# A fp32 attention and two feed-forward nets on TensorE: output places, token places and deferred sums held by other times, and more steps with seven products

## The chip, the cores and the metric

The kernel runs on one core of a Trainium2 chip. The metric is the device time of the whole kernel in microseconds (us), the median of several runs. All times below are in us unless marked ns.

## The reference

Attention over channels (a 256 x 256 score matrix) on 6016 tokens, then two feed-forward nets with 256 -> 2048 -> 256 features, all in fp32:

```python
qn = q / (norm(q, axis=1) + 1e-06);  kn = k / (norm(k, axis=1) + 1e-06)
s = kn.T @ qn / tau                                   # 256 x 256
a = exp(s - s.max(-1));  a /= a.sum(-1) + 1e-09
x = v @ a                                             # 6016 x 256
h = x @ moe_w_in;   x = (h / (1 + exp(-h))) @ moe_w_out
h = x @ moe2_w_in;  out = maximum(0.01 * h, h) @ moe2_w_out
```

## The kernel before

**Stages.** The first 60 us read q and k, make the score matrix and the softmax, and fold it into the first weights, so that net one works on v itself. Net one (`moe` 1) and net two (`moe` 2) fill the rest. Their tokens are cut into six pairs of halves, `tpairs`: five of 2 x 512 and one of 2 x 448. For each net and each pair, written (net, pair) as (2,1), there are eight steps `s`; a step makes two of the sixteen blocks of 128 hidden features for both halves of the tokens, and adds them, times w_out, into four PSUM banks `ps_y`, one for each pair of an output block `m` and a token half.

**Products.** TensorE (PE) multiplies fp32 values as high and low parts: each product is three matmuls, hi x hi, hi x lo and lo x hi, called a triplet here. The first layer of a step (`product`, L477, into ps_a, ps_b and ps_d) makes 2 x 2 blocks with seven products M1 to M7 instead of eight, with sums on VectorE (DVE) and ScalarE (ACT): DVE's `da` (L561) adds into ps_d, `d22` (L581) makes a block of hidden values `hs`. After the activation (ACT L488, L490) each block is split: ACT casts the high part `gh` (L123), DVE subtracts for the low part `gl` (`lows`, L504).

The second layer (L650) of a plain step has eight products (`l2`). In a step with seven (`l2_seven`) the hidden blocks are first combined into sums T1 and T2 (DVE, L600) and T3 and T4 (transfers on POOL's queue that add in memory, L613), and P1 to P7 take them with w_out or with sums of w_out blocks (`wsh`, `wsl`). P2, P3, P4 and, in pairs whose last step is plain, P5 go into ps_y directly. P1, P6, P7 and otherwise P5 are chained over the steps of a batch in the bank ps_x, which DVE copies or adds to E1, E2, E3 or E5 in SBUF (`keep`, L712) and later adds into ps_y (`close`, L723). `SECOND` and `BATCHES` (L65, L66) say which steps of a pair are seven and how they are batched; without an entry in `BATCHES` a pair of net two takes `SECOND`.

**End of a pair.** `finish` (L732) brings each of the four banks to SBUF as `o`: in net one with an addition or a copy (L740, L743) and a transfer to `y_d` in memory (L745); in net two by a transpose (L747) and four transfers each to the output (L753), on SP's queue, sixteen for a pair.

**Places.** `hs`, `gh`, `gl`, the tokens `xf`, `xh`, `xl`, the loaded `v_raw`, `E` and `o` lie in a common set of places of 128 x 512 fp32 in SBUF. `take` pops the first of the list `free`, and who is done puts a place back at its end. An instruction that gets a place still being read waits for the reader.

**Order.** A planner (L1178 to the end of the kernel function) sets the order on all engines: every piece is a `Work` with an engine, a cost, the works it waits for, a due time `at` in steps, an earliest step `release`, and the number of places it needs (`homes`, `spare`). It takes the work that can start first by its own estimate, with a delay `LATE` after each engine, and looks at the first 48 of each queue. Works on the queue "none" have no instruction; they take or free places. `new_x` (L158) takes the places of the next pair's tokens and gives back those of the pair before the last.

Of the kernel before, what the change touches and what calls it, by code (L numbers as in the profile page):

```python
# [15 lines left out]
P = 128  # L16
# [3 lines left out]
def attention_moe_kernel(  # L20
# [44 lines left out]
    SECOND = ((0, 1, 2, 3), (4, 5, 6))  # L65
    BATCHES = {(1, 3): ((2, 4), (5, 6)), (1, 4): ((0, 1), (2, 4), (5, 6)), (1, 5): ((0, 1), (2, 4), (5, 6))}  # L66
# [91 lines left out]
    def new_x(qi, n=7):  # L158
        if qi > 1:
            for a in (xh, xl):  # L160
                free.extend(x[0] for x in a.pop(qi - 2) if x)
        xf[qi] = [take(F32, "xf") for _ in range(n)] + [None] * (7 - n)
        xh[qi], xl[qi] = [None] * 7, [None] * 7
# [567 lines left out]

    def finish(moe, p, m, half):  # L732
# [3 lines left out]
        free.append(i)  # L736
        if moe == 1:
            if batches(moe, p):
                name = last_add(moe, p, m, half)
                nc.vector.tensor_tensor(out=o[:, :n], in0=ps, in1=kept[p, name][1][:, :n], op=ALU.add)  # L740
                fed_on(p, name, own_fifth(moe, p))
            else:
                nc.vector.tensor_copy(out=o[:, :n], in_=ps)  # L743
            y_d[p, m, half] = dram.tile([P, n], F32, tag=f"y{p}{m}{half}", name="y_d")
            nc.sync.dma_start(out=y_d[p, m, half], in_=o[:, :n])  # L745
            return
        nc.vector.transpose(out=o[:, :n], in_=ps)  # L747
# [7 lines left out]
    def drop_x(qi):  # L755
        for a in (xh, xl):
            free.extend(x[0] for x in a.pop(qi) if x)

    with tc.manual_schedule():
# [365 lines left out]
        WIDTHS = {"i": 7 * HG, "o": FG * C, "s": 3 * P, "f": 3 * P, "a": P}  # L1125
# [22 lines left out]
        ENDING = ("P1", "P5", "P6", "P2", "P7", "P3", "P4")  # L1148
# [7 lines left out]
        def open_more():  # L1156
            decode.close()
            more_pool[0] = ctx.enter_context(tc.tile_pool(name="spool", bufs=1))
            last_pool = ctx.enter_context(tc.tile_pool(name="hpool", bufs=1))
            spots.update({i: last_pool for i in range(HOMES, HOMES + 2)})  # L1160
            free.extend(range(HOMES, HOMES + 2))
# [28 lines left out]
        rel, last_x = {}, None  # L1190
# [19 lines left out]
        def prepare_out(g, dep, at):  # L1210
            s1 = dep
            for x in (2 * g, 2 * g + 1):
# [8 lines left out]
            return done  # L1221
# [45 lines left out]
        def tokens(qi):  # L1267
# [3 lines left out]
            old = [o for (a, kk), o in ONES.items() if kk // SS == qi - 2]  # L1271
            new = Work("none", 0, lambda eng: new_x(qi, 4), old, release=k - 0.5, homes=4, spare=2)
            got = []
            for x, (kc, half) in enumerate(blocks):
                if qi < NP:
                    ld = Work("sp", 0.4, lambda eng, a=(qi, kc, half): load_v(*a), [new], release=k + x // 2, homes=1, spare=6)
# [4 lines left out]
            def form(i, deps, keeps=False, frees=()):  # L1281
                h = Work("act", sc(n), lambda eng: x_hi(qi, i, eng), deps, homes=2, spare=6)
# [52 lines left out]
        def first(k):  # L1335
# [11 lines left out]
            if qi == 2 * NP - 1 and s == 0:  # L1347
                Work("none", 0, lambda eng: drop_x(2 * NP - 2), [o for (a, kk), o in ONES.items() if kk // SS == qi - 1])
# [13 lines left out]
            def split(form, deps, free_deps=()):  # L1362
                h = Work("act", sc(n), lambda eng: cast(step, form, eng), deps, homes=1)
# [23 lines left out]
            else:  # L1387
# [7 lines left out]
                ready["T2"] = split("T2", [t2])  # L1395
                ready["T3"] = split("T3", [t3])
# [4 lines left out]
        def add(k):  # L1401
# [5 lines left out]
            wdeps = W2.get(g, []) if moe == 2 else W2.get(("first", s, "s"), W2["first", g])  # L1407
# [76 lines left out]
            if s == SS - 1:  # L1484
                for m in range(KC):
                    for half in range(2):
                        o = Work("dve", tt(n), lambda eng, a=(moe, p, m, half): finish(*a), ends[qi, m, half] + extra.get((qi, m, half), []), homes=1, at=k + 1.5 + half / 2)
                        FIN[qi, m, half] = after_fin[m, half] = o
# [16 lines left out]
        while left:  # L1505
            best = None
            for e, q in queues.items():
                q[:48] = [o for o in q[:48] if o.end is None]
                mine = None
                for o in q[:48]:  # L1510
# [16 lines left out]
            clock[e] = t + cost  # L1527
# [41 lines left out]
```

## Time and profile before

| | before |
|---|---|
| median of 3 runs | 1013.74 us (1013.54 to 1014.42) |
| the profiled execution | 1013.32 us |
| its span, first to last instruction | 1011.3 us |
| mean granted TensorE clock | 0.998 |
| busy: PE, DVE, ACT, POOL | 996.6, 836.1, 768.3, 161.1 us |

The profiled execution is one run; its span leaves out what lies before the first and after the last instruction. A busy time is the union of an engine's instructions. Two matmuls overlap in the profile (each lasts 0.39 us, but the next starts 0.23 us later), so the pace of PE is read from starts and its halts from longer distances between starts. A line of busy time by stage has the stretch, its length, then the busy time and number of instructions of PE, PEld (loads of weights, which overlap PE), DVE, ACT and POOL, the granted clock (1.00 is full speed), the share of the DMA engines and GB/s; in the chain of waits each line is a start, a length and what ran or was under way, "SPq" being SP issuing a transfer.

### The profile page before, as it was taken

How to read it: one execution, taken by the hardware profiler on the slowest of the kernel's cores; microseconds unless marked ns; L12 is line 12 of the kernel's file. 1: busy time of each engine (PE TensorE's matmuls, PEld its weight loads, DVE VectorE, ACT ScalarE, POOL GpSimd, SP SyncE). 2: the span in 40 equal slices, each digit the busy share in tenths (PEclk: the TensorE clock that was granted, in tenths of full speed). 3: DMA queues.
4: the chain of work that ended last, by engine and by line, in shares of the span. 5: the costliest groups of instructions: out<-in, count | busy, mean ns of one | idle time of the engine just before them, and what ended most of it. 6: DMA issues, size and time to landing. Idle time of an engine off the chain costs nothing.

```text
span 1011.3 us, 13654 instructions
## 1 busy us (share of the span) xinstructions
PE 996.6 (99%) x4450; PEld 830.1 (82%) x4450; DVE 836.1 (83%) x1432; ACT 768.3 (76%) x1427; POOL 161.1 (16%) x207
## 2 busy tenths in 40 slices
PE   8999999999999999999999999999999999999997
PEld 7878888887888888888998888888788788888996
DVE  5889887988898778888878888888788888888876
ACT  6888756877787777777876887887787797787774
POOL 2300000000001231211334221221120221121220
PEclk9999999999999999999999999999999999999999
DMA  9734625556548455423789643542533533442533
GB/s 352 292 107 133 150 67 170 177 168 162 208 172 193 116 104 94 98 46 78 198 229 312 142 84 74 95 82 68 100 64 83 96 71 78 84 81 43 91 55 61
DMA packets 152088, 128.38 MB, mean 127 GB/s; under 512 B 97488, under 2 KB 114384, under 8 KB 152016
## 3 DMA queue, kind: packets, MB, share of 16 engines
q1 hardware_dynamic: 120944, 74.93, 25.1%
q0 software_dynamic: 27360, 52.11, 25.0%
q10 hardware_dynamic: 3712, 0.46, 0.3%
q8 instruction: 35, 0.57, 0.2%
q14 instruction: 37, 0.30, 0.1%
HBM read 60.95 MB, written 31.85 MB: 92 GB/s over the span
## 4 chain that ended last, share of the span: by engine, by line
PE 85%; DMA 5%; DVE 4%; SPq 2%; ACT 2%; issue 1%; DVEq 0%; ACTq 0%; POOLq 0%
PE ps_y L650 31%; PE ps_a L477 22%; PE ps_x L650 12%; PE ps_d L477 11%; PE ps_b L477 5%; PE ps_h L477 3%; DMA k_raw<-in_k_dram 2%; SPq L753 2%; DVE gl L504 1%; PE w_ps L384 1%; DMA q_raw<-in_q_dram 1%; DMA w_raw<-in_moe_w_in_dram 1%; DMA hs<-hs 1%; DMA out_dram<-o 1%; SPq L791 0%
## 5 line engine op out<-in xcount | busy, mean ns | idle before, releaser
L504 DVE TENSOR_TENSOR gl<-hs,gh 128x512 fp32r<-128x512 f32 (+1 forms) x558 | 363.9, 673 | 74.5 <-ACT gh L123 66.0
L123 ACT CAST gh<-hs 128x512 fp32r<-128x512 f32 (+1 forms) x558 | 324.1, 610 | 6.7 <-DMA hs<-hs 0.8
L650 PE MATMUL ps_y<-gh,wol 128*128 128x512 f32 (+1 forms) x462 | 178.5, 386 | 0.5 <-DVE wol L355 0.5
L650 PE MATMUL ps_y<-gh,woh 128*128 128x512 f32 (+1 forms) x462 | 178.6, 387 | 0.2 <-DVE ps_y L723 0.2
L650 PE MATMUL ps_y<-gl,woh 128*128 128x512 f32 (+1 forms) x462 | 178.6, 387 | 0.0
L613 POOL DMA_DIRECT2D hs<-hs x116 | 100.9, 912 | 483.1 <-DVE gl L504 144.6
L477 PE MATMUL ps_a<-xh,wch 128*128 128x512 f32 (+1 forms) x352 | 137.3, 390 | 3.5 <-DVE ps_d L561 2.3
L477 PE MATMUL ps_a<-xl,wch 128*128 128x512 f32 (+1 forms) x352 | 135.7, 385 | 0.0
L477 PE MATMUL ps_a<-xh,wcl 128*128 128x512 f32 (+1 forms) x352 | 135.6, 385 | 0.0
L650 PEld LDWEIGHTS ps_y<-gh,wol 128*128 128x128 f32 x462 | 86.7, 188 | 17.7 <-DVE wol L355 0.9
L650 PEld LDWEIGHTS ps_y<-gh,woh 128*128 128x128 f32 x462 | 86.7, 188 | 17.2 <-DVE ps_y L723 0.5
L650 PEld LDWEIGHTS ps_y<-gl,woh 128*128 128x128 f32 x462 | 86.7, 188 | 16.9 <-DVE gl L504 0.3
L581 DVE TENSOR_TENSOR hs<-ps_a,c 128x512 f32<-128x512 f32 (+1 forms) x88 | 59.5, 676 | 37.4 <-PE ps_a L477 36.4
L600 DVE TENSOR_TENSOR hs<-hs 128x512 f32<-128x512 f32 (+1 forms) x116 | 78.1, 673 | 10.3 <-ACT hs L490 5.0
L477 PEld LDWEIGHTS ps_a<-xh,wch 128*128 128x128 f32 x352 | 66.0, 188 | 22.0 <-DVE ps_d L561 4.9
L477 PEld LDWEIGHTS ps_a<-xh,wcl 128*128 128x128 f32 x352 | 66.1, 188 | 12.4
L477 PEld LDWEIGHTS ps_a<-xl,wch 128*128 128x128 f32 x352 | 66.1, 188 | 11.3
L561 DVE TENSOR_TENSOR ps_d<-ps_a,c 128x512 f32<-128x512 f32 (+1 forms) x88 | 60.1, 683 | 14.7 <-PE ps_a L477 13.7
L477 PE MATMUL ps_d<-xh,wch 128*128 128x512 f32 (+1 forms) x176 | 67.9, 386 | 0.0
L477 PE MATMUL ps_d<-xh,wcl 128*128 128x512 f32 (+1 forms) x176 | 67.8, 385 | 0.0
L477 PE MATMUL ps_d<-xl,wch 128*128 128x512 f32 (+1 forms) x176 | 67.8, 385 | 0.0
L192 POOL DMA_DIRECT2D xf<-xf x20 | 17.8, 897 | 313.7 <-DVE xl L126 198.7
(149 smaller groups left out, 1810.5 us busy)
## 6 DMA issues: line engine op xcount, KB each, us to landing
hs<-hs POOLq DMA_DIRECT2D x90, 256.0 KB, 3.2
w_d<-st SPq DMA_DIRECT2D x40, 256.0 KB, 3.1
w_raw<-in_moe_w_in_dram SPq DMA_DIRECT2D x16, 512.0 KB, 4.3
w_raw<-in_moe_w_out_dram SPq DMA_DIRECT2D x16, 512.0 KB, 3.7
hs<-hs POOLq DMA_DIRECT2D x26, 224.0 KB, 3.2
y_d<-o SPq DMA_DIRECT2D x20, 256.0 KB, 2.6
xf<-y_d SPq DMA_DIRECT2D x20, 256.0 KB, 3.5
out_dram<-o SPq DMA_DIRECT2D x80, 64.0 KB, 2.3
```

What stands on the lines that cost most here:

```text
L123: nc.scalar.copy(out=hi, in_=src)
L192: nc.gpsimd.dma_start(out=at(put), in_=at(M6), accum_op=ALU.add)
L384: nc.tensor.matmul(ps, lhsT=a[:, jc, m * P:(m + 1) * P], rhs=b[jc], start=(x == 0), stop=(x == len(order) - 1),)
L477: nc.tensor.matmul(ps[:, :n], lhsT=a, rhs=b, start=(start and x == 0), stop=(x == 2), skip_group_check=not start,)
L504: nc.vector.tensor_tensor(out=lo[1], in0=h[1], in1=f32(got[0][1]), op=ALU.subtract)
L561: nc.vector.tensor_tensor(out=got["D"][:, :n], in0=got["A"][:, :n], in1=got["c5"], op=ALU.add)
L581: nc.vector.tensor_tensor(out=hs[step, "22"][1], in0=got["A"][:, :n], in1=got["c5"], op=ALU.add)
L600: nc.vector.tensor_tensor(out=out[1], in0=hs[step, a][1], in1=hs[step, b][1], op=ALU.subtract)
L613: nc.gpsimd.dma_start(out=hs[step, part][1], in_=hs[step, "T2"][1], accum_op=ALU.add)
L650: nc.tensor.matmul(ps, lhsT=a, rhs=b, start=(first and x == 0), stop=(last and x == 2), skip_group_check=True,)
L753: queues[j % len(queues)].dma_start(out=dst[j], in_=src[j * BL:(j + 1) * BL])
```

## The change

It does the following.

1. In net two, step 7 becomes a step with seven products in pairs (2,0) to (2,4), in the batches (0,1,2,3) and (4,5,6,7). Pair (2,5) keeps its plain last step. In net one, pairs (1,4) and (1,5) have seven such steps instead of six, in two batches instead of three. (1,3) stays as it is.
2. The place of an output `o` is put back in `free` not by `finish` but by a new work `leave` on SP, which issues the transfers; its cost is 0.5 (net one) or 2.4.
3. Token places are given back one product at a time after their true last use (`drop_x`), the next tokens' places are taken 3.5 steps later (`XA`), the loads of v are spread over half a step each, and their high parts wait until `k + XB`.
4. The casts of T2 and T3 are planned only at the end of their batch (`TURN`), so that the sum holds one place until then, not `gh` and `gl` two.
5. Two extra places are gone (`hpool`).
6. For (2,5) a half of w_out that step 7's sums overwrite is stored before and loaded again ("r").
7. P3 comes earlier in the last step of a batch (`ENDING`), and the planner looks at all works of "none", whose clock stays at 0.

```diff
-    SECOND = ((0, 1, 2, 3), (4, 5, 6))
-    BATCHES = {(1, 3): ((2, 4), (5, 6)), (1, 4): ((0, 1), (2, 4), (5, 6)), (1, 5): ((0, 1), (2, 4), (5, 6))}
+    SECOND = ((0, 1, 2, 3), (4, 5, 6, 7))
+    TURN, XA, XB = 1.1, 3.0, 5.0
+    BATCHES = {(2, 5): ((0, 1, 2, 3), (4, 5, 6)), (1, 3): ((2, 4), (5, 6)), (1, 4): ((0, 1, 2, 3), (4, 5, 6)), (1, 5): ((0, 1, 2, 3), (4, 5, 6))}
...
-        if qi > 1:
-            for a in (xh, xl):
-                free.extend(x[0] for x in a.pop(qi - 2) if x)
...
+    going = {}
+
     def finish(moe, p, m, half):
         r0, n = tpairs[p]
         ps = accs.pop((p, m, half))[:, :n]
         i, o = take(F32, "o")
-        free.append(i)
+        going[moe, p, m, half] = i, o
...
+    def leave(moe, p, m, half):
+        r0, n = tpairs[p]
+        i, o = going.pop((moe, p, m, half))
+        free.append(i)
+        if moe == 1:
             y_d[p, m, half] = dram.tile([P, n], F32, tag=f"y{p}{m}{half}", name="y_d")
             nc.sync.dma_start(out=y_d[p, m, half], in_=o[:, :n])
             return
...
-    def drop_x(qi):
+    def drop_x(qi, i):
         for a in (xh, xl):
-            free.extend(x[0] for x in a.pop(qi) if x)
+            if a[qi][i]:
+                free.append(a[qi][i][0])
...
-        ENDING = ("P1", "P5", "P6", "P2", "P7", "P3", "P4")
+        ENDING = ("P1", "P3", "P5", "P6", "P2", "P7", "P4")
...
-            last_pool = ctx.enter_context(tc.tile_pool(name="hpool", bufs=1))
-            spots.update({i: last_pool for i in range(HOMES, HOMES + 2)})
-            free.extend(range(HOMES, HOMES + 2))
...
+            raw = []
+            for x in (2 * g, 2 * g + 1):
+                if x in returning:
+                    a = x % 2 * C + P
+                    s1 = stage(("r", x, 0), P, lambda a=a: wo_f[g][:, a:a + P], [s1], at)
+                    raw.append(s1)
...
-            old = [o for (a, kk), o in ONES.items() if kk // SS == qi - 2]
-            new = Work("none", 0, lambda eng: new_x(qi, 4), old, release=k - 0.5, homes=4, spare=2)
+            last = {a: o for (a, kk), o in ONES.items() if kk == k - 1}
+            drops = [
+                Work("none", 0, lambda eng, a=a: drop_x(qi - 2, xs[a]), [last.get(a)], at=k - 1.0) for a in xs
+            ] if qi > 1 else []
+            new = Work("none", 0, lambda eng: new_x(qi, 4), drops, release=k + XA, homes=4, spare=2)
             got = []
             for x, (kc, half) in enumerate(blocks):
                 if qi < NP:
-                    ld = Work("sp", 0.4, lambda eng, a=(qi, kc, half): load_v(*a), [new], release=k + x // 2, homes=1, spare=6)
+                    ld = Work("sp", 0.4, lambda eng, a=(qi, kc, half): load_v(*a), [new], release=k + XA + x / 2, homes=1, spare=6)
...
-                h = Work("act", sc(n), lambda eng: x_hi(qi, i, eng), deps, homes=2, spare=6)
+                h = Work("act", sc(n), lambda eng: x_hi(qi, i, eng), deps, release=k + XB, homes=2, spare=6)
...
+                for x in returning:
+                    ms = slice(x % 2 * C + P, x % 2 * C + C)
+                    W2["last", x] = [load(
+                        ("r", x), lambda x=x, ms=ms: (flat(woh[x // 2])[:, ms], flat(wol[x // 2])[:, ms]), users[2, x], k + 1
+                    )]
+                for a in xs:
+                    Work("none", 0, lambda eng, a=a: drop_x(2 * NP - 2, xs[a]), [ONES[a, k - 1]], at=k - 1.0)
...
-                ready["T2"] = split("T2", [t2])
-                ready["T3"] = split("T3", [t3])
+                wait = batch(step)[-1] - s
+                ready["T2"] = split("T2", [t2], release=k + wait + TURN if wait else 0.0)
+                ready["T3"] = split("T3", [t3], release=k + wait + TURN if wait else 0.0)
...
-                        FIN[qi, m, half] = after_fin[m, half] = o
+                        after_fin[m, half] = o
+                        FIN[qi, m, half] = Work(
+                            "sp", 0.5 if moe == 1 else 2.4, lambda eng, a=(moe, p, m, half): leave(*a), [o], at=k + 1.6 + half / 2, late=-2.4
+                        )
...
-                q[:48] = [o for o in q[:48] if o.end is None]
+                seen = 48 if e != "none" else len(q)
+                q[:seen] = [o for o in q[:seen] if o.end is None]
...
-            clock[e] = t + cost
+            clock[e] = t + cost if e != "none" else 0.0
```

What it moves, at two places of the order. The first is DVE at the end of pair (2,1), before the change, from the last of the four finishes on. `gl`, `gh`, `hs`, `o` are places with a running number; "waits DMAHW..." means that the instruction waits for transfers that SP issued, "DMASW" for POOL's.

```order
L747 STREAM_TRANSPOSE o_7570<-ps_y_6826 128x512 [waits PE_49]
L561 TENSOR_TENSOR ps_d_7515<-ps_a_7538,c5_7534 128x512 [waits PE_49,Activation_49]
L504 TENSOR_TENSOR gl_7584<-hs_7483,gh_7542 128x512 [waits Activation_49]
L581 TENSOR_TENSOR hs_7597<-ps_a_7538,c5_7534 128x512 [waits PE_49]
L504 TENSOR_TENSOR gl_7604<-hs_7589,gh_7595 128x512 [waits Activation_49]
L504 TENSOR_TENSOR gl_7611<-hs_7474,gh_7602 128x512 [waits DMASW0_49,Activation_49]
L600 TENSOR_TENSOR hs_7613<-hs_7613,hs_7589 128x512 [waits Activation_49]
L504 TENSOR_TENSOR gl_7627<-hs_7513,gh_7618 128x512 [waits DMASW1_49,Activation_49]
L504 TENSOR_TENSOR gl_7635<-hs_7597,gh_7625 128x512 [waits DMAHW4_49,DMAHW5_49,DMAHW3_49,DMAHW6_49,DVE_49,Activation_49]
L600 TENSOR_TENSOR hs_7597<-hs_7613,hs_7597 128x512 [waits DVE_49]
L504 TENSOR_TENSOR gl_7652<-hs_7613,gh_7637 128x512 [waits Activation_49]
L504 TENSOR_TENSOR gl_7665<-hs_7629,gh_7658 128x512 [waits DMAHW5_49,DMAHW4_49,DMAHW6_49,DMAHW3_49,Activation_49]
```

And the same place of the changed kernel, from the last two finishes on:

```order
L745 STREAM_TRANSPOSE o_7663<-ps_y_6965 128x512 [waits DVE_49]
L745 STREAM_TRANSPOSE o_7668<-ps_y_6904 128x512 [waits DMAHW5_49,DMAHW4_49,DMAHW6_49,DMAHW3_49,DVE_49]
L598 TENSOR_TENSOR hs_7518<-hs_7535,hs_7518 128x512
L502 TENSOR_TENSOR gl_7685<-hs_7643,gh_7661 128x512 [waits Activation_49]
L502 TENSOR_TENSOR gl_7695<-hs_7535,gh_7636 128x512
L502 TENSOR_TENSOR gl_7702<-hs_7678,gh_7693 128x512 [waits Activation_49]
L598 TENSOR_TENSOR hs_7655<-hs_7655,hs_7613 128x512
L598 TENSOR_TENSOR hs_7643<-hs_7655,hs_7643 128x512 [waits DVE_49]
L502 TENSOR_TENSOR gl_7723<-hs_7655,gh_7717 128x512 [waits Activation_49]
L559 TENSOR_TENSOR ps_d_7674<-ps_a_7681,c5_7687 128x512 [waits PE_49]
L502 TENSOR_TENSOR gl_7749<-hs_7730,gh_7743 128x512 [waits Activation_49]
L579 TENSOR_TENSOR hs_7756<-ps_a_7681,c5_7687 128x512 [waits PE_49]
```

Before, the eighth and the eleventh instruction after the last finish are gl ops that take places of `o` and wait for its transfers, and the second of them stands two ahead of the next ps_d. In the changed order only the last finish waits for a transfer, that of the first `o` of the pair, which was filled 15 instructions before (L745 at row 1004 of DVE's order, against 1019); the next gl that waits for output transfers is 17 instructions behind the last finish, at row 1036. From the first finish of (2,1) to that of (2,2) DVE has 109 instructions, before 105.

The second place is PE at the end of step 7 of (2,1). Before the change (plain products of the step, with first-layer products of the next pair between them):

```order
L650 MATMUL ps_y_6849<-gh_7453,woh_5979 128x512
L650 MATMUL ps_y_6849<-gl_7476,woh_5979 128x512
L650 MATMUL ps_y_6849<-gh_7453,wol_5980 128x512
L477 MATMUL ps_a_7538<-xh_7155,wch_5192 128x512
L477 MATMUL ps_a_7538<-xl_7156,wch_5192 128x512
L477 MATMUL ps_a_7538<-xh_7155,wcl_5193 128x512
L650 MATMUL ps_y_6798<-gh_7456,woh_5979 128x512
L650 MATMUL ps_y_6798<-gl_7493,woh_5979 128x512
L650 MATMUL ps_y_6798<-gh_7456,wol_5980 128x512
L650 MATMUL ps_y_6826<-gh_7456,woh_5979 128x512
L650 MATMUL ps_y_6826<-gl_7493,woh_5979 128x512
L650 MATMUL ps_y_6826<-gh_7456,wol_5980 128x512
```

And in the changed kernel:

```order
L648 MATMUL ps_x_7252<-gh_7493,wsh_6016 128x512
L648 MATMUL ps_x_7252<-gl_7511,wsh_6016 128x512
L648 MATMUL ps_x_7252<-gh_7493,wsl_6017 128x512
L475 MATMUL ps_d_7567<-xh_7213,wch_5233 128x512
L475 MATMUL ps_d_7567<-xl_7214,wch_5233 128x512
L475 MATMUL ps_d_7567<-xh_7213,wcl_5234 128x512
L475 MATMUL ps_a_7574<-xh_7221,wch_5233 128x512
L475 MATMUL ps_a_7574<-xl_7222,wch_5233 128x512
L475 MATMUL ps_a_7574<-xh_7221,wcl_5234 128x512
L648 MATMUL ps_x_7252<-gh_7504,wsh_5882 128x512
L648 MATMUL ps_x_7252<-gl_7532,wsh_5882 128x512
L648 MATMUL ps_x_7252<-gh_7504,wsl_5883 128x512
```

Before, the step's last products go into ps_y with `woh` and `wol` and end the sum. In the change P6 of step 7 (`wsh_6016`) ends a chain in ps_x, two first-layer triplets follow, and P7 of step 4 begins the next chain in the same bank, with DVE's copy to E2 in between. Over the whole kernel PE has 21 matmuls fewer, DVE 35 instructions more (21 gl, 14 of T1 and T2, eight of sums of w_out, fewer additions of E), ACT 25 more (21 gh), POOL 22 transfers more (14 of T3 and T4, eight loads of weights) and SP eight stores more.

## Rows read from the trace of the kernel before

**Rows 1.** The page: the span, and busy time, share and count of each engine.

```profile
span 1011.3 us, 13654 instructions
PE 996.6 (99%) x4450; PEld 830.1 (82%) x4450; DVE 836.1 (83%) x1432; ACT 768.3 (76%) x1427; POOL 161.1 (16%) x207
```

**Rows 2.** Busy time by stage; two pairs of net two.

```profile
642.00:720.00 78.00, 77.47 (x341) 63.48 (x339) 65.66 (x105) 61.55 (x114) 12.99 (x16) 1.00 0.43 82
720.00:798.00 78.00, 77.29 (x339) 63.41 (x339) 65.35 (x106) 60.28 (x112) 14.01 (x17) 1.00 0.42 81
```

**Rows 3.** The chain of waits 700 to 722: start, length, what; first and last of fourteen triplets.

```profile
701.09 1.39 PE ps_y L650 x6
...
709.95 0.68 PE ps_b L477 x3
```

**Rows 4.** The chain of waits 965 to 985: first and last of 24 triplets.

```profile
970.15 0.61 PE ps_a L477 x3
...
984.14 0.61 PE ps_a L477 x3
```

**Rows 5.** Timeline of PE at three pair ends: start, length, instruction, idle time before.

```profile
719.08 0.39 PE L650 MATMUL ps_y<-gh,wsl 128*128 128x512 f32 x1
720.71 0.50 PE L477 MATMUL ps_a<-xh,wch 128*128 128x512 f32 x1 [1.24 <-DVE ps_d L561]
721.05 0.40 PE L477 MATMUL ps_a<-xl,wch 128*128 128x512 f32 x1
...
797.72 0.39 PE L650 MATMUL ps_y<-gh,wsl 128*128 128x512 f32 x1
798.59 0.50 PE L477 MATMUL ps_a<-xh,wch 128*128 128x512 f32 x1 [0.48 <-DVE ps_d L561]
...
875.54 0.39 PE L650 MATMUL ps_y<-gh,wsl 128*128 128x512 f32 x1
876.32 0.50 PE L477 MATMUL ps_a<-xh,wch 128*128 128x512 f32 x1 [0.39 <-DVE ps_d L561]
```

**Rows 6.** Waits of PE, 140 to 1011, and one of DVE, 600 to 1011: us, times, longest.

```profile
PE ps_a L477 <- DVE ps_d L561: 2.3, 4, 1.2
PE ps_a L477 <- ACT ps_b L555: 0.8, 2, 0.5
PE ps_a L477 <- ACT c L555: 0.2, 1, 0.2
PE ps_a L477 <- DVE hs L581: 0.2, 1, 0.2
PE ps_y L650 <- DVE ps_y L723: 0.2, 1, 0.2
...
DVE gl L504 <- DMA out_dram<-o: 2.0, 2, 1.6
```

**Rows 7.** The chain of waits 700 to 722, from SP's output transfers to PE.

```profile
713.49 0.49 SPq L753
...
716.19 0.49 SPq L753
...
716.73 1.91 DMA out_dram<-o
...
718.75 1.29 DVE gl L504 x2
720.04 0.62 DVE ps_d L561
```

**Rows 8.** Timeline of DVE, 773 to 776.

```profile
773.17 0.68 DVE L504 TENSOR_TENSOR gl<-hs,gh 128x512 fp32r<-128x512 f32 x1
773.77 0.69 DVE L723 TENSOR_TENSOR ps_y<-ps_y,E 128x512 f32<-128x512 f32 x1
```

**Rows 9.** Timeline of ACT, 245 to 253.

```profile
251.94 0.62 ACT L123 CAST gh<-hs 128x512 fp32r<-128x512 f32 x1 [0.73 <-DMA y_d<-o]
```

**Rows 10.** The chain of waits 530 to 546.

```profile
533.69 6.80 DMA hs<-hs
```

## What the change will do to the time: the prediction

> **What bounds the kernel now.** I read the page's busy times first: TensorE works for 996.6 of the 1011.3 us of the span, VectorE for 836.1, ScalarE for 768.3 [rows 1]. By stage it is the same: in two stretches of 78 us, each about one token pair of net two, PE is busy for 77.3 and 77.5 us, DVE for 65.4 and 65.7, ACT for 60.3 and 61.6, at a granted clock of 1.00 [rows 2]; that is the upper of the two levels, 2.4 GHz, so no clock is to be won. The time is therefore the number of matmuls times their spacing, plus the places where PE stands still.
>
> The spacing comes from the chain of waits. Between 701.09 and 709.95 the fourteen triplets (three matmuls of 512 columns) take 9.54 us, 0.68 each [rows 3]; in the last pair, with 448 columns, 24 triplets from 970.15 to 984.75 take 14.60 us, 0.61 each [rows 4].
>
> The halts come from the starts of neighbouring matmuls, against 0.227 us (a third of 0.68). At the end of pair (2,1) the step from 719.08 to 720.71 is 1.40 us too long, and the next, from 720.71 to 721.05, 0.11, since the first matmul after a halt is slow; at (2,2), 797.72 to 798.59, it is 0.64, at (2,3), 875.54 to 876.32, 0.55, and I add the 0.11 there too [rows 5]: 1.51 + 0.75 + 0.66 = 2.92 us in all. The list of waits names ps_d (L561) on DVE for PE, and, on DVE, gl (L504) behind a transfer of `o` to the output [rows 6]. The chain at 719 has the links: SP issues the pair's sixteen output transfers, about 0.54 us apart, the last at 716.73; that one lands after 1.91 us, at 718.64; two gl ops follow, then ps_d from 720.04, and PE at 720.71 [rows 7]. A gl was given the place of an `o` still under way, and DVE takes its work in order, so ps_d stood behind it.
>
> **Part 1, matmuls: -4.70 us.** A step with seven products has one triplet fewer than a plain one. Step 7 becomes seven in the five pairs (2,0) to (2,4), one step in (1,4), one in (1,5); (2,5) and (1,3) keep theirs. Six triplets of 512 columns, 6 x 0.68 = 4.09, and one of 448, 0.61 [rows 3, 4]: 4.70 us. All lie on PE, which the stage rows show to be full, so they come off the span whole unless a wait takes their room. The TensorE page of the Trainium skill ("TensorE: Matmul & The Clock Gate", section "Wait — 56ns, not 53.3ns?") states about N / 2.4 GHz + 2.5 ns from start to start, 215.7 ns at 512 columns; by that this part would be an estimated 4.45 us, but the rows have 227 ns and decide.
>
> **Part 2, output places: -2.92 us.** A place is now free for the planner only when the new work on SP that sends `o` has been planned, with its true delay. In the order of the changed kernel at the end of (2,1) the fourth finish takes the place of the first `o`, 15 DVE ops after it was filled, and the first gl on such a place comes 17 ops after the last finish. At 0.60 us an op [rows 8] these are 9 and 10 us; four issues and a landing need 4 x 0.54 + 1.91 = 4.1 us, eight issues 6.2 [rows 7]. So both waits should find their transfer landed, at all three pair ends, and 2.92 us go. What is late next there: the sums. E2 has to be copied out of ps_x between the chains of P6 and P7, with two other triplets, 1.36 us, between them. The same hand-over stands in the middle of each pair today, and the list of PE's waits has no ps_x in it [rows 6].
>
> **Part 3, work added on other engines: 0 in the sum.** Between two pairs' first finishes DVE has 109 ops in the new order against 105. At the busy time per op of the stage rows (65.66 / 105 = 0.625) [rows 2] that is 68.2 us, under the 76.3 that PE's 112 triplets take (112 x 0.681). ACT gets three casts more per seven step, 0.62 each [rows 9]: 61.6 + 1.9 = 63.5. Both are covered by PE as long as the backlog in front of ps_d stays short. The casts of T2 and T3 now wait for the end of their batch (they hold one place instead of two meanwhile), so up to eight gl ops come close together there; the same place holds for net one. The bound is zero where they fit between PE's needs, and 1.2 us at a batch end where they do not, the longest wait of PE on ps_d [rows 6]. I take zero, since DVE has 8 us of idle time left per pair.
>
> **Part 4, x places, loads, weights: 0, bounds -2.2 and +2.** Loads of v are spread instead of issued together. At 251.94 an ACT cast waited 0.73 us for a y_d transfer [rows 9], the net-one form of the same thing, and ACT's copy into ps_b behind it held PE: 0.8 us in two places [rows 6]. PE's listed waits after 140 us come to 3.7 us; the three pair ends make 1.24 + 0.48 + 0.39 = 2.1 of it [rows 5, 6], and as measured by the starts they were 2.92, 1.4 times that. The other 1.6 us would by the same factor be 2.2: the better bound. Against it, the first forms of x are made later, nearer to the step that needs them; there are two places fewer; and in (1,5) the weights of net two and the T3 and T4 transfers on POOL's queue (two more for each new seven step) crowd together. One such transfer, issued at 533.69, took 6.80 us to land [rows 10]; ACT's cast of its sum came late and PE then waited 0.2 us for ACT's c [rows 6]; if four such transfers cost PE its longest wait on ACT, 0.5 us [rows 6], each, that is the +2. I take zero between them, the value nearest to both kinds of row. The half of w_out that is kept for (2,5) and the sums of the new steps add eight stores on SP and eight loads on POOL; where the DMA engines are 0.42 to 0.43 busy [rows 2] they cost nothing, and without that cover one load would be late once, at the worst by those 6.80 us. The planner's own changes (how far it looks, its clock for "none") have no instruction.
>
> **Sum.** 1011.3 - 4.70 - 2.92 = 1003.7 us of span. The profiled execution lasted 1013.32, 2.0 more than its span, and lies 0.42 under the median of 1013.74; the same two differences give 1013.74 - 7.62 = **1006.1 us**. About 0.2%, 2 us, is what a measurement of this kernel can tell from no change.
>
> **Rivals.**
> *The matmuls only.* The three waits go but come back in smaller pieces: the pair end now has four P6, four P7, the keeps, five closing additions and four finishes close together, and the next pair's first products need the banks of the finishes. For it: PE's one listed wait on ps_y is for such a closing addition (L723), at the end of the last pair [rows 6]; against it, it is 0.2 us, and the order leaves two triplets or more between each such pair of works. If as much comes back as went, 1013.74 - 4.70 = 1009.0.
>
> *Halts at every batch end, slower.* The bunched casts of T2 and T3 put ps_d behind a row of gl ops, each of which also waits for its cast on ACT. There are ten batch ends in the five changed pairs of net two. At 1.2 us each [rows 6] they cost 12 us: 1013.74 - 7.62 + 12 = 1018.1. The point from which it decides: with (7.62 + 2.0) / 10 = 0.96 us lost at each, the kernel is slower by 0.2%. For it: two gl ops, begun late at 718.75, were enough to give PE 1.51 us of halt [rows 5, 7]. Against it: in the new order some fifteen DVE ops, 9.0 us at 0.60, stand beside the twelve triplets of the bunch, 8.2 us, so DVE falls back by 0.8 us at most, under the 0.96.
>
> *VectorE becomes the bound.* If each op cost its shown duration of 0.68 us [rows 8] and nothing overlapped, 109 ops would be 74.1 us, and with DVE's own waits for ACT over PE's 76.3; the pairs of net two would then stay as long as they are, and only net one's two triplets, 1.29 us, would go: 1012.4. Against it: successive ops start 0.60 us apart, though each shows 0.68 [rows 8]. The VectorE page of the Trainium skill ("VectorE: DVE Perf Modes", section "The TRN2 errata") gives (N + 151) / 0.96 GHz for a single fp32 tensor_tensor, 691 ns at 512 elements; taken per op that would be an estimated 75.3 us of a pair. The duration agrees with the trace, but the starts are closer than that, and they decide.
>
> *More gained.* With part 4's better bound, 1006.1 - 2.2 = 1003.9; where the slow starts of the smaller halts go too, about another 1.1 us (ten times 0.11), 1002.8.
>
> **How the numbers follow.** The forecast, 1004.5 to 1007.8, 0.52; the matmuls only, 1007.8 to 1011, 0.24; more gained, 0.10; VectorE bound, 0.04; halts at every batch end, 0.10, of which 0.04 stays within 0.2% and 0.06 beyond. Faster by over 0.2% (under 1011.7): 0.52 + 0.24 + 0.10 = 0.86; within 0.2%: 0.04 + 0.04 = 0.08; slower: 0.06. The range from 1002.8 to 1010.5 holds the first three but for their edges, about 0.83.
>
> **What would show it.** 21 matmuls fewer on PE; 76.3 us from the first finish of one net-two pair to that of the next; in the list of waits no gl behind an output transfer from 640 us on, and PE's wait on ps_d down from 2.3 us to a few tenths. Wrong would be: PE waiting for ps_d, ps_y or ps_x at each pair's end or middle for over 0.3 us; DVE above 70 of 76 us; or a longer stretch between 200 and 560 us, where the new places and loads work.

## The result, and the profile after

The changed kernel takes 1019.48 us (median of 4 runs, 1018.22 to 1020.13) against 1014.03 for the kernel before in the same comparison: a ratio of 1.0052, 95% interval 1.0035 to 1.007. It is slower, where 1006.1 was predicted.

The page of the changed kernel, as [rows 1] for the one before:

```profile
span 1017.4 us, 13736 instructions
PE 995.9 (98%) x4429; PEld 827.1 (81%) x4429; DVE 851.7 (84%) x1467; ACT 777.2 (76%) x1452; POOL 177.2 (17%) x229
```

PE has its 21 matmuls fewer, yet the span is 6.1 us longer. Line numbers differ a little between the two kernels: L475, L502, L559, L579 and L648 of the changed one are L477, L504, L561, L581 and L650 of the one before; SP's outputs are L760 for L753, its loads of x L214 for L216, DVE's first sum of x L188 for L190. By stage, as [rows 2]:

```profile
642.00:720.00 78.00, 76.74 (x338) 62.89 (x337) 68.60 (x110) 62.12 (x116) 15.45 (x18) 1.00 0.45 87
720.00:798.00 78.00, 75.41 (x326) 61.71 (x325) 66.14 (x107) 60.28 (x113) 13.78 (x17) 0.98 0.45 85
```

In the second stretch PE makes 326 matmuls where it made 339. DVE is at 66 to 69 of 78 us, so it is not full. The lists of waits, of PE from 140 us on and (last line) of DVE from 640 us on; total, times, longest:

```profile
PE ps_a L475 <- DVE ps_d L559: 6.6, 6, 2.6
PE ps_a L475 <- DVE hs L579: 1.2, 2, 0.8
PE ps_d L475 <- ACT hs L486: 0.7, 1, 0.7
PE ps_y L648 <- DVE gl L502: 0.4, 2, 0.2
PE ps_a L475 <- ACT ps_b L553: 0.3, 1, 0.3
PE ps_y L648 <- ACT gh L124: 0.2, 1, 0.2
...
DVE xf L188 <- DMA xf<-y_d: 7.2, 4, 2.9
```

Against [rows 6], gl no longer waits for an output, as forecast, but PE's wait on ps_d has grown from 2.3 to 6.6 us, and DVE has a new wait: its sum of the next pair's x (L188) for the transfer that loads it from `y_d`. The chain of waits of the changed kernel has the links at the longest of the four:

```profile
723.79 1.13 ACT hs L488 x2
724.92 0.58 SPq L214
...
725.60 4.81 DMA xf<-y_d
...
730.51 0.09 DVE xf L188
...
731.12 0.68 DVE gl L502
731.80 0.62 DVE ps_d L559
...
732.46 1.65 PE ps_a L475 x3
```

SP is held at the second of the four loads until ACT (L488) is done at 724.91, issues the third at 725.60, and this one lands after 4.81 us; L188 starts, then a gl and ps_d, and PE goes on at 732.46. Why the loads are issued so late is seen on SP. First the kernel before, then the changed one (start, length, instruction, number):

```profile
693.39 1.78 SPq L216 DMA_DIRECT2D xf<-y_d  x4
706.20 11.03 SPq L753 DMA_DIRECT2D out_dram<-o  x16
```

```profile
707.23 15.33 SPq L760 DMA_DIRECT2D out_dram<-o  x16
722.72 4.35 SPq L214 DMA_DIRECT2D xf<-y_d  x4
```

Before, the four loads of a pair's x ran 13 us ahead of the sixteen outputs; in the change they stand behind them in SP's queue, since their places are taken 3.5 steps later. The finishes of the pair start at 706.5, 709.5, 714.9 and 715.5 (705.5 to 708.6 before), since each waits for its closing additions; SP waits for them in turn, and the outputs hold it for 15.33 us. The loads then take 4.35 us to issue where they took 1.78, since some of their places are still in use. SP's waits from 575 to 960 us, which hold four pairs, have for them (the last time is the longest wait):

```profile
SPq L214 <- ACT hs L488: 3.6, 4, 1.2
SPq L214 <- DMA hs<-hs: 3.0, 2, 1.6
SPq L214 <- ACT gh L124: 1.1, 4, 0.4
```

That is about 2 us a pair. The larger part is the place in the queue: even the first load, which is issued at 722.72, lands at 728.69, when L188 could have started at 727.61. The reader has moved too: L188 stands 16 DVE instructions behind the last finish, where L190 stood 25 or 28 behind it.

The halts of PE (distance from start to start above 0.227 us, or 0.202 at 448 columns, where it is over by more than 0.04), added up by stretch from the starts in the trace of one execution each:

| | 140 to 470 us | 470 to 580 | 580 to the end | all |
|---|---|---|---|---|
| before | 3.10 | 1.04 | 3.68 | 7.82 |
| changed | 2.92 | 4.04 | 10.77 | 17.74 |

9.92 us of halts more, less 4.70 us of triplets, make 5.2; PE's last matmul starts 5.5 us later (1005.48 and 1010.94). The rest of the longer span lies behind it.

### The profile page after: what moved, and what is told of

Its sections match the earlier page's. It is cut to its first block, busy times and chain, and to the rows that moved or that the text cites. A ratio compares the mean times of both kernels' runs of the same rounds, so it can differ in the third digit from the quotient of the medians.

```text
span 1017.4 us, 13736 instructions
## 1 busy us (share of the span) xinstructions
PE 995.9 (98%) x4429; PEld 827.1 (81%) x4429; DVE 851.7 (84%) x1467; ACT 777.2 (76%) x1452; POOL 177.2 (17%) x229
## 4 chain that ended last, share of the span: by engine, by line
PE 80%; DMA 9%; DVE 5%; ACT 3%; issue 1%; SPq 1%; POOL 0%; DVEq 0%; POOLq 0%; ACTq 0%
PE ps_y L648 29%; PE ps_a L475 20%; PE ps_x L648 11%; PE ps_d L475 10%; PE ps_b L475 5%; PE ps_h L475 3%; DMA xf<-y_d 2%; DMA hs<-hs 2%; DMA k_raw<-in_k_dram 2%; DVE gl L502 1%; ACT gh L124 1%; DMA q_raw<-in_q_dram 1%; PE w_ps L382 1%; DMA w_raw<-in_moe_w_in_dram 1%; ACT hs L488 1%
## 5 line engine op out<-in xcount | busy, mean ns | idle before, releaser
L502 DVE TENSOR_TENSOR gl<-hs,gh 128x512 fp32r<-128x512 f32 (+1 forms) x579 | 375.3, 673 | 57.1 <-ACT gh L124 51.4
L124 ACT CAST gh<-hs 128x512 fp32r<-128x512 f32 (+1 forms) x579 | 335.0, 611 | 20.9 <-DVE hs L598 8.0
L611 POOL DMA_DIRECT2D hs<-hs x130 | 112.3, 919 | 493.1 <-DVE gl L502 154.1
L648 PE MATMUL ps_y<-gl,woh 128*128 128x512 f32 (+1 forms) x439 | 169.9, 387 | 0.4 <-DVE gl L502 0.4
L648 PE MATMUL ps_y<-gh,woh 128*128 128x512 f32 (+1 forms) x439 | 169.8, 387 | 0.4 <-ACT gh L124 0.2
L648 PE MATMUL ps_y<-gh,wol 128*128 128x512 f32 (+1 forms) x439 | 169.6, 386 | 0.5 <-DVE wol L353 0.5
L475 PE MATMUL ps_a<-xh,wch 128*128 128x512 f32 (+1 forms) x352 | 138.0, 392 | 8.2 <-DVE ps_d L559 6.6
L475 PE MATMUL ps_a<-xl,wch 128*128 128x512 f32 (+1 forms) x352 | 135.9, 386 | 0.0
L475 PE MATMUL ps_a<-xh,wcl 128*128 128x512 f32 (+1 forms) x352 | 135.8, 386 | 0.0
L648 PEld LDWEIGHTS ps_y<-gl,woh 128*128 128x128 f32 x439 | 82.5, 188 | 17.2 <-DVE gl L502 1.3
L648 PEld LDWEIGHTS ps_y<-gh,woh 128*128 128x128 f32 x439 | 82.5, 188 | 17.1 <-ACT gh L124 0.8
L598 DVE TENSOR_TENSOR hs<-hs 128x512 f32<-128x512 f32 (+1 forms) x130 | 87.5, 673 | 10.5 <-ACT hs L486 4.6
L648 PEld LDWEIGHTS ps_y<-gh,wol 128*128 128x128 f32 x439 | 82.4, 188 | 16.6 <-DVE wol L353 1.0
L579 DVE TENSOR_TENSOR hs<-ps_a,c 128x512 f32<-128x512 f32 (+1 forms) x88 | 59.5, 676 | 40.6 <-PE ps_a L475 39.9
L475 PEld LDWEIGHTS ps_a<-xh,wch 128*128 128x128 f32 x352 | 66.1, 188 | 28.5 <-DVE ps_d L559 10.6
L475 PEld LDWEIGHTS ps_a<-xh,wcl 128*128 128x128 f32 x352 | 66.2, 188 | 12.3
L475 PEld LDWEIGHTS ps_a<-xl,wch 128*128 128x128 f32 x352 | 66.3, 188 | 11.3
L559 DVE TENSOR_TENSOR ps_d<-ps_a,c 128x512 f32<-128x512 f32 (+1 forms) x88 | 59.9, 680 | 12.8 <-PE ps_a L475 11.7
L190 POOL DMA_DIRECT2D xf<-xf x20 | 17.9, 989 | 294.4 <-DVE ps_d L559 170.8
L475 PE MATMUL ps_d<-xh,wch 128*128 128x512 f32 (+1 forms) x176 | 68.2, 388 | 0.7 <-ACT hs L486 0.7
L475 PE MATMUL ps_d<-xl,wch 128*128 128x512 f32 (+1 forms) x176 | 68.0, 386 | 0.0
L475 PE MATMUL ps_d<-xh,wcl 128*128 128x512 f32 (+1 forms) x176 | 68.0, 386 | 0.0
```

Of the source, the lines that this page charges most:

```text
L124: nc.scalar.copy(out=hi, in_=src)
L190: nc.gpsimd.dma_start(out=at(put), in_=at(M6), accum_op=ALU.add)
L475: nc.tensor.matmul(ps[:, :n], lhsT=a, rhs=b, start=(start and x == 0), stop=(x == 2), skip_group_check=not start,)
L502: nc.vector.tensor_tensor(out=lo[1], in0=h[1], in1=f32(got[0][1]), op=ALU.subtract)
L559: nc.vector.tensor_tensor(out=got["D"][:, :n], in0=got["A"][:, :n], in1=got["c5"], op=ALU.add)
L579: nc.vector.tensor_tensor(out=hs[step, "22"][1], in0=got["A"][:, :n], in1=got["c5"], op=ALU.add)
```

## The experiments

Theory A: the four halts in net two, near 651, 729, 811 and 889 us, are the late load under an early reader: loads behind the outputs, the sum of them 16 DVE instructions behind the last finish, ps_d behind the sum. Theory B is the prediction's own rival, DVE too full by the bunched casts. All times are medians; each ratio is to the kernel before on the same chip. Runs e1 to e4 ran on one chip and e5 to e11 on another, so runs are compared by their ratios (0.1% is 1.0 us). Each ratio is uncertain by about 0.1%, so a difference of two of them below 0.15% to 0.2% says little by itself.

### e1 and e2: the reader later, or the load earlier

e1 moves DVE's sum alone, from 16 to 40 instructions behind the last finish:

```diff
-            s5 = Work("dve", tt(n), lambda eng: x_form(qi, M5), got)
+            s5 = Work("dve", tt(n), lambda eng: x_form(qi, M5), got, release=k + XS if qi >= NP else 0.0)
```

with `XS = 4.5`.

> The changed kernel with one due time added: DVE's first sum of the next pair's x in net two (L188) may be placed only 4.5 steps after the previous pair has begun, so it stands 40 DVE instructions behind the last finish instead of 16; loads, outputs and all else keep their order. Theory A (a late load under an early reader): the four halts near 651, 729, 811 and 889 us, 8.5 us by the starts with the slow clock behind the second, are DVE standing in that sum for the reloaded x, with ps_d behind it; they go, and the median falls from 1019.5 to about 1011, the list of waits showing no DVE xf behind xf<-y_d. Theory B (DVE is too full where the casts of T2 and T3 are bunched, and ps_d comes late in any case): less than 2 us is won, 1017.5 or more, and PE goes on waiting for ps_d at the same places.

e2 moves the loads alone, ahead of the outputs; the sum stays 16 instructions behind the last finish:

```diff
-            new = Work("none", 0, lambda eng: new_x(qi, 4), drops, release=k + XA, homes=4, spare=2)
+            new = Work("none", 0, lambda eng: new_x(qi, 4), drops, release=k + (XA if qi < NP else -0.5), homes=4, spare=2)
```

> The changed kernel with the places of net two's next x taken at the old release (k - 0.5), so that SP issues the four loads of a pair ahead of the previous pair's sixteen output transfers; DVE's sum L188 keeps its place 16 instructions behind the last finish. Theory A: the loads have long landed when the sum starts, the four halts go as in the run with the later sum, about 1011. Theory B: as the DVE order is the same, the halts stay, 1017.5 or more. If the loads hold places that others need, new waits of DVE or ACT on a place show as well.

Measured: e1 1011.76 us, ratio 0.9976 (0.9965 to 0.9987); e2 1010.76 us, ratio 0.9965 (0.9953 to 0.9977). Either edit alone takes 0.76% and 0.87% off the changed kernel, 7.7 and 8.8 us, and makes it faster than the kernel before. SP of e2, and behind it of e1:

```profile
687.94 2.35 SPq L214 DMA_DIRECT2D xf<-y_d  x4
705.20 15.57 SPq L760 DMA_DIRECT2D out_dram<-o  x16
```

```profile
704.72 16.59 SPq L760 DMA_DIRECT2D out_dram<-o  x16
721.47 3.37 SPq L214 DMA_DIRECT2D xf<-y_d  x4
```

In e1 the load is as late as in the changed kernel and does no harm, because nobody asks for it yet. In e2 the list of PE's waits from 575 us on is empty; in e1 it has one line:

```profile
PE ps_y L648 <- DVE ps_y L721: 0.2, 1, 0.2
```

Halts after 580 us fall from 10.77 to 2.27 (e1) and 1.86 us (e2). Theory A holds. Theory B falls: in e2 the 1467 instructions of DVE stand in the sequence of the changed kernel, bunched casts and all, and so do those of PE, ACT and POOL; only SP's differ, from 480 us on, and PE's list has no wait there. No run leaves the places as late and moves the loads to another queue, so how the 8.5 us divide between the outputs ahead of the loads and the places still in use is told by the rows above alone.

The same comparison shows how far one execution's halts can be relied on. Up to 480 us e2 has the changed kernel's order on every engine, yet 4.43 us of halts before 470 where that one has 2.92: a load of v landed after 6.54 us and PE stood for 1.39 us at 355, which it did not in the changed kernel. So 1.5 us between two such sums, in net one, can be chance.

### e3, e7 and e9: the new steps of net one

```diff
-    BATCHES = {..., (1, 4): ((0, 1, 2, 3), (4, 5, 6)), (1, 5): ((0, 1, 2, 3), (4, 5, 6))}
+    BATCHES = {..., (1, 4): ((0, 1), (2, 4), (5, 6)), (1, 5): ((0, 1), (2, 4), (5, 6))}
```

e3 puts this on e1, e7 on e2. e9 keeps all new steps and gives (1,5) the batches (0,1), (2,3), (4,5,6), on e8 (below). The place in question in the changed kernel, in its chain of waits:

```profile
536.72 8.30 DMA hs<-hs
...
545.05 0.57 ACT gh L124
...
545.64 0.62 DVE gl L502
546.27 0.61 DVE ps_d L559
```

A transfer of T3 or T4 needs 8.30 us to land, at a stretch (540 to 550 us) in which the DMA engines are 1.10 busy (the times of the packets that start there, as a share of the time of 16 engines). Before, the one of 6.80 us [rows 10] fell in a stretch (530 to 540 us) of 0.99.

> The kernel with the later sum, and pairs (1,4) and (1,5) back to six steps with seven products in three batches. Two triplets come back, 0.68 + 0.61 = 1.29 us. Theory C (the new steps of (1,5) put their T3 and T4 transfers among the loads of net two's weights, and PE's halts from 499 to 574 us, 3.9 us against 1.0 before, are their late landing): about 1.6 us faster than the run with the later sum, with the halts there back to about 1 us. Rival (the stretch is full of transfers either way and halts come with both): 1.3 us slower than that run.

> The kernel with the early loads, and pairs (1,4) and (1,5) back to six steps with seven products in three batches. Theory C (T3 and T4 transfers late among loads of net two's weights): PE's halts between 490 and 575 us, 2.9 us in e2, fall under 1, against 1.29 us of triplets that come back: about 1.5 us faster than e2, 1009.3. Rival, as e3 left it open: the halts go but others of the same size come in net one, so that the time is that of e2 or up to 1.3 us more.

> The kernel e8 (early loads, v loads from step 1), and pair (1,5) with its seven steps in the batches (0,1), (2,3), (4,5,6) instead of (0,1,2,3), (4,5,6); no triplet comes back. The first blocks of w_out are then used up two steps earlier and net two's weights can be loaded over them earlier. Theory C, narrowed to (1,5): the 2.9 us that PE loses from 543 to 556 us in e8 (a T3/T4 transfer of about 8 us among weight loads) fall under 1.5, and the time from 1008.4 to about 1006.8. Rival (the stretch holds too many transfers wherever they stand): the halts stay or move, 1008 to 1009.5.

Measured: e3 1011.46 us, 0.9970 (0.9958 to 0.9982), the same as e1. Its halts from 470 to 580 us fall from 2.76 to 0.07 us, but those from 140 to 470 rise from 3.08 to 5.14, and the triplets come back. Two halts, 1.51 us at 279 and 1.66 us at 356, make most of the 5.14, and the second is at the place at which e2 has 1.39 us and the changed kernel none. e7 1013.95 us, 0.9999 (0.9990 to 1.0008), 0.34% slower than e2, more than the two triplets: from 470 to 580 us it still has 2.03 us, partly at other places, and there is a new halt of 1.24 us at 621; the whole 0.34% is not accounted for. e9 1008.44 us, 0.9953 (0.9941 to 0.9965), the same as e8, with 3.61 us there instead of 2.65. So theory C is not confirmed as a way to gain: with the tables of e3 and e7 the planner orders net one anew from about 180 us on, with that of e9 from 490 us on, and the halts move. That such transfers land late there and hold PE is seen; which arrangement would avoid it stays open.

### e4 and e10: the output places

e4 is e1 with the places freed by `finish` again; e10 is the kernel before with `leave` alone. The lines of e10 that call it (`finish` and `leave` themselves are as in the change):

```diff
-                        FIN[qi, m, half] = after_fin[m, half] = o
+                        after_fin[m, half] = o
+                        FIN[qi, m, half] = Work(
+                            "sp", 0.5 if moe == 1 else 2.4, lambda eng, a=(moe, p, m, half): leave(*a), [o], at=k + 1.6 + half / 2, late=-2.4
+                        )
```

> The kernel with the later sum, and the place of an output freed by finish again, with the transfers issued there, as before the change. The prediction's part 2 (a place freed too early made gl wait for the output transfer at pair ends): halts at the pair ends come back, up to 2.9 us slower than the run with the later sum, with gl behind out_dram<-o in the list of waits. Rival (with more free places at pair ends the first in the list come so late that the early freeing costs nothing): within 0.5 us of it.

> The kernel before, with the output places alone changed: finish keeps the place, a work on SP sends the output and puts the place back. The prediction's part 2 by itself: the halts at the ends of (2,1), (2,2) and (2,3) go, 2.9 us faster than before (1010.8 for 1013.7), no gl behind out_dram<-o there. Rival (fewer free places at the pair ends, or the loads of the next x now planned behind the outputs, bring other waits of the same size): within 1 us of before, or slower.

Measured: e10 1010.99 us, ratio 0.9975 (0.9966 to 0.9984), 2.7 us faster than the 1013.73 beside it; the prediction had 2.92. Halts after 580 us fall from 3.68 to 1.00 us, and DVE's list from 600 us on has no gl behind an output, where [rows 6] had 2.0 us. PE at the end of (2,1) in e10, where [rows 5] had 1.63 us from start to start:

```profile
719.02 0.39 PE L650 MATMUL ps_y<-gh,wsl 128*128 128x512 f32 x1
719.24 0.45 PE L477 MATMUL ps_a<-xh,wch 128*128 128x512 f32 x1
719.53 0.40 PE L477 MATMUL ps_a<-xl,wch 128*128 128x512 f32 x1
```

e4: 1013.04 us, 0.9993 (0.9981 to 1.0005), 0.17% slower than e1, with intervals that overlap, and its twelve runs spread more (1011.06 to 1017.08 us; e1 1009.53 to 1014.73). The old halts at the pair ends don't come back there; the profile has another, once, at 726 us, 20 us behind a pair's last product, behind an output that took 5.20 us to land:

```profile
721.77 5.20 DMA out_dram<-o
...
727.20 0.70 DVE gl L502
...
727.95 0.73 PE ps_y L648 x2
```

So the term was right for the order it was worked out from. In the changed order early freeing costs less, if anything; that more places are free there is a possible reason, which was not tried.

### e5: the matmul term

e2 with the old `SECOND` of net two, so that step 7 of (2,0) to (2,4) is plain:

```diff
-    SECOND = ((0, 1, 2, 3), (4, 5, 6, 7))
+    SECOND = ((0, 1, 2, 3), (4, 5, 6))
```

> The kernel with the early loads (e2), and step 7 of pairs (2,0) to (2,4) plain again as before the change (loads ahead of the outputs, everything else of the change kept): the matmul term of the prediction by itself. If the five removed triplets come off the path whole, 5 x 0.68 = 3.4 us slower than e2, 1014.2, and 76.4 us from pair end to pair end in e2 against 77.1 here. Rival (the crowded pair end with its chains, closing additions and finishes takes the room back): less than 1.5 us slower, with PE waiting at the pair ends of e2 only.

Measured: 1012.72 us, ratio 0.9988 (0.9979 to 0.9996), 0.23% or 2.3 us slower than e2, between the two theories; by the intervals, about 1.5 us either way, it can't exclude 3.4 nor 1.5. The profiles tell more. From the first finish of a net-two pair to that of the next it is 76.1 to 76.6 us in e2 (76.3 was predicted) and 76.5 to 76.9 in e5, at each of the four pairs 0.3 to 0.5 more, so a triplet less is worth about 0.4 us of its 0.68. They also say where the rest is. In e5 no halt over 0.04 us is left between 560 and 989 us; e2 has, at each end of a pair with a seven last step, one like this at (2,2):

```profile
781.86 0.39 PE L648 MATMUL ps_x<-gh,wsl 128*128 128x512 f32 x1
782.23 0.50 PE L475 MATMUL ps_a<-xh,wch 128*128 128x512 f32 x1
782.56 0.40 PE L475 MATMUL ps_a<-xl,wch 128*128 128x512 f32 x1
```

0.37 and 0.33 us instead of 0.227: 0.25 us at each of four such ends, 0.19 at the fifth, 1.2 us in all. 3.4 less 1.2 is 2.2, near the 2.3 of the medians. What holds PE there was not tried; the list of waits does not name it.

### e6: the bunched casts

```diff
-                wait = batch(step)[-1] - s
+                wait = 0
```

> The kernel with the early loads, and the casts of T2 and T3 of a batch's earlier steps not held until the end of the batch, so each holds two places instead of one. If the bunched casts cost PE something (the prediction's slower rival), this is faster than e2 by over 1 us in net two; if they fit between PE's needs, it is the same within 0.7 us, or slower where fewer free places make gl or gh wait for a place (DMA or PE named as releaser of gl).

Measured: 1011.52 us, ratio 0.9985 (0.9976 to 0.9994), 0.20% slower than e2, with intervals that just touch. Halts after 580 us rise from 1.86 to 5.28 us; the list of PE's waits from 575 us on, empty in e2, has two, the second for the copy of E out of ps_x:

```profile
PE ps_a L475 <- ACT ps_b L553: 0.7, 1, 0.7
PE ps_x L648 <- DVE E L710: 0.5, 1, 0.5
```

So holding the casts back does not cost, and by the medians it pays. Why is not shown: the expected waits for a place are not in DVE's list, and the planner orders all engines but SP anew from 347 us on. The rival by which I had the kernel slower was wrong in its mechanism: in e2 the casts are bunched and PE's list is empty.

### e8 and e11: the v loads of net one

e8 is e2 with `XA` = 1.0 for net one, e11 with -0.5:

```diff
-    TURN, XA, XB = 1.1, 3.0, 5.0
+    TURN, XA, XB = 1.1, 1.0, 5.0
```

> The kernel with the early loads, and in net one the places and loads of v taken 1 step after the start of the previous pair instead of 3. In e2 PE lost 1.4 us at 355 us where a v load took 6.54 us to land and DVE's transposes of it (L207) stood ahead of gl. If late v loads are the like of the late y loads: the halt at 355 us goes and with it a spread of the runs, 1 to 1.5 us faster than e2 (1009.5). Rival (that landing is chance, other waits in net one are of DVE and ACT themselves): within 0.5 us of e2.

> The kernel e8 with the v loads of net one, too, at the old release (k - 0.5, spread by half a step each). If it is only lateness that the later loads cost, this is like e8, 1008.4 within 0.7. If early loads crowd SP and the places at pair ends, as the old 244 and 252 us halts suggested, it is slower than e8 by 0.7 to 2 us, with PE waiting near 240 to 260 us.

Measured: e8 1008.44 us (1007.88 to 1009.40), ratio 0.9950 (0.9937 to 0.9962), 0.15% faster than e2, with intervals that overlap: halts from 140 to 470 us fall from 4.43 to 2.32 us, and the 1.39 us at 355 is gone. But the changed kernel, with the order of e2 there, had no such halt either (2.92 us in all), so these profiles do not show that the earlier load removed it. e8 is faster than both kernels. e11 1010.53 us, 0.9970 (0.9958 to 0.9981), 0.20% slower than e8, with intervals that just overlap and 4.87 us of halts there. The largest, 1.94 us at 246 us with 1.6 us of the lower clock behind it, is where it was expected, but the chain that leads to it has no load: ps_d stands behind a row of DVE's work on weights (`w_f`, `w_r`, `st`). So these runs do not show that early loads crowd anything; e8, e2 and e11 differ in the planner's order, from 158 us on, and by little in time. The page of e8:

```profile
span 1006.1 us, 13769 instructions
PE 992.9 (99%) x4429; PEld 827.4 (82%) x4429; DVE 851.5 (85%) x1467; ACT 775.6 (77%) x1452; POOL 177.7 (18%) x229
```

## Why the prediction was wrong

**The step that failed** is part 4, "x places, loads, weights: 0, bounds -2.2 and +2". I named that x is formed later and nearer to its use, but priced only v in net one and the transfers of (1,5). I did not follow net two's four loads past the sixteen outputs on SP, nor ask how far behind the last finish their first reader stands. Both stand in the order of the instructions: loads behind the outputs, the reader 16 DVE instructions after the last finish, about 9.6 us at 0.60 [rows 8] and 11.4 in the trace (716.2 to 727.6), while SP issues the loads only after all outputs, from 722.7 on, and they land 4.4 to 6.0 us after their issue there. The halts it made are 8.5 us by the starts, the lower clock behind the second one included; undoing either half of it gave 7.7 and 8.8 us (e1, e2). The bound of +2 was far too near, since it came from rows of another transfer. Of the better bound, -2.2, nothing is seen: 2.92 us of halts from 140 to 470 us against 3.10. In sum the span was to shrink by 7.62 us and grew by 6.1; the late loads (8.5), the transfers of (1,5) (3.0) and the new pair ends (1.2) make 12.7 of the 13.7 between.

**Part 1** was right in the number of triplets and in that they come off the path. Net of the new pair ends, 0.25 us each, which I had at zero, the five of net two are worth 2.2 us by the profiles of e2 and e5 instead of 3.4.

**Part 2** was right: -2.92 predicted, -2.7 measured alone (e10). In the changed kernel the old halts are gone, with 0.25 us in their place.

**Part 3** was right in its zero for DVE, and the bunching that I feared costs nothing (e2; e6 is 0.20% slower without it, at the edge of the noise). In e2, between 640 and 960 us, DVE is 70 to 72 of 80 us busy, and PE's list has no wait.

**The transfers of (1,5)**, in part 4 with a bound of +2, cost 3.0 us more halts from 470 to 580 us (4.04 against 1.04) in the changed kernel's profile, but 1.7 and 1.5 us in those of e1 and e2, which have the same steps; e3, e7 and e9 move these halts but don't settle them.

**The rivals.** "Halts at every batch end" had the right side and the right instruction at the end of the chain, ps_d, but the wrong cause and places: four halts of 1.2 to 2.8 us, 22 us after a pair's last product, not ten at batch ends. With the loads of both nets moved (e8) the change is worth 0.50%, 5.1 us, of the 7.6 forecast, with those of net two alone (e2) 0.35%. In e8's profile the time from the first to the last matmul shrinks by 5.8 us: 4.70 of triplets and 1.1 of halts. The halts end at 6.73 us against 7.82: less 1.9 us after 580 and 0.8 before 470, but 1.6 more from 470 to 580.

## What to carry to other kernels

When a change moves the time at which places are taken or given back, follow each load that needs them: where it now stands in its queue, how long what is ahead of it holds the queue (here outputs that wait for their own producers), and how many instructions of its first reader's engine lie between. A reader planned too early turns a late load into a halt of all that stands behind it on its engine, here ps_d behind L188, even if what it makes is not needed for a while; planning it later did as well here as loading earlier (e1, e2). Price a move by the queue it passes, not by the halts that the old order happens to show.

## What the runs showed of the hardware

After the longest halt the clock fell. PE of the changed kernel around 729 us, in its timeline:

```profile
729.49 0.39 PE L475 MATMUL ps_b<-xh,wcl 128*128 128x512 f32 x1
...
732.46 0.79 PE L475 MATMUL ps_a<-xh,wch 128*128 128x512 f32 x1 [2.59 <-DVE ps_d L559]
733.05 0.63 PE L475 MATMUL ps_a<-xl,wch 128*128 128x512 f32 x1
733.48 0.63 PE L475 MATMUL ps_a<-xh,wcl 128*128 128x512 f32 x1
```

and by windows:

```profile
729.00:736.00 7.00, 4.41 (x14) 3.20 (x13) 3.78 (x6) 1.79 (x4) 0.85 (x1) 0.76 0.53 119
```

PE had nothing to do for 2.59 us; then matmuls start 0.43 us apart until 735.2 instead of 0.227, the lower of the two levels, 1.2 GHz, with a mean granted clock of 0.76 in these 7 us. That made 1.5 us on top of a halt of 2.75 us. In the three shorter halts of its kind (1.2 to 1.4 us too long) the spacing after them is 0.227 us again. Two halts of e11 (1.94 us at 246 and 2.09 us at 545) were followed by a stretch of 0.43 us too, one of 2.00 us in e9 (at 542) was not, so in these runs the length of a halt alone does not tell whether the clock falls.

A halt costs 0.1 us more than its wait: in nearly all of them the first matmul behind it, of 512 columns, is followed after 0.33 to 0.34 us instead of 0.227, as in [rows 5] from 720.71 to 721.05.
